# Linear attention, mixture of experts and a gelu layer on one core: one low half moved to GpSimd, one diagonal to ScalarE

## The chip, the cores and the metric

The kernel runs on one core of a Trainium2 chip. A core has TensorE (PE in the rows; its weight loads are PEld), VectorE (DVE), ScalarE (ACT), GpSimd (POOL) and SyncE (SP, which only issues DMAs here). Each engine works through its own list of instructions in order; they wait for one another by semaphores. The metric is device time in microseconds. The kernel before takes 1238.77 us, the median of three runs from 1238.41 to 1241.19.

## The reference

Three layers follow one another: softmax attention in its linear form (4 batches, 8 heads, 576 rows, head size 64), a mixture of four experts with relu (2304 rows, width 512, hidden width 1024), and a dense layer with a gelu (hidden width 2048).

```python
def _attn_ref(q, k, v) -> np.ndarray:
    q_s = q - np.max(q, axis=-1, keepdims=True)
    q_s = np.exp(q_s)
    q_s = q_s / (np.sum(q_s, axis=-1, keepdims=True) + 1e-09)
    k_s = k - np.max(k, axis=2, keepdims=True)
    k_s = np.exp(k_s)
    k_s = k_s / (np.sum(k_s, axis=2, keepdims=True) + 1e-09)
    kv = np.einsum('bhsd,bhse->bhde', k_s, v)
    return np.einsum('bhsd,bhde->bhse', q_s, kv).astype(np.float32)
...
    for e in range(E):
        h = np.maximum(x @ w1[e], 0.0)
        out += p[:, e:e + 1] * (h @ w2[e])
...
def _moe2_ref(x, w_in, w_out) -> np.ndarray:
    h = x @ w_in
    g = h * (1.0 / (1.0 + np.exp(-1.702 * h)))
    return (g @ w_out).astype(np.float32)
```

The row of key maxima, `np.max(k, axis=2)`, is a maximum over the 576 rows of a head. The expert layer's relu, `np.maximum(x @ w1[e], 0.0)`, and the gelu `g` are what the changed lines work on.

## The kernel before

All products run on TensorE in a format with a shortened mantissa, so each operand is split into a high half (a copy in that format) and a low half (the value less its high half), and each product is three: high by high, high by low, low by high. The splitting of weights, inputs and hidden activations is the work of the other three engines.

The expert layer and the gelu layer are cut into units of 256 hidden columns. The rows are in three groups of 2 x 512, 2 x 256 and 2 x 384. In the first pass of a layer the units run one after another on group 0 (`i == 0`): 13 such steps in the expert layer (the first three units are done another way) and 8 in the gelu layer. In the second pass the units run on groups 1 and 2. In a step, seven products of blocks (`m1` to `m7`, line 837) give the four tiles of the hidden activation in the manner of Strassen: `a` (from `py` or `p1`), `b` (from `u3`), `c` (from `px`) and `d` (from `pz` or `u2`). For group 0 three of the four lie in PSUM; only `b`, the tile `u` of the rows, is in SBUF: `u3c` copies `px` there by ScalarE and `u3a` adds `pz` by VectorE (line 868). Then `r` makes the high half (line 881: relu on ScalarE; in the gelu layer a gelu at 877 and a cast at 883) and `l` the low half (lines 887 and 891, both on VectorE).

The second product (`mm2`, line 954) takes eight row tiles in a step, into banks of `pso` in PSUM (`po`). VectorE adds each into `acc` (line 968, gelu layer 975 and 977), which gives the bank back. Four of the tiles of a step run at the word `TILES`, at the end of the next step, and four at `REST`, early in the step after that. Tile `b` belongs to the half of the rows that `REST` takes.

The order of work is written by hand: `STAGES` lists, for five stages, the operations of this step and (with a minus) of the one before. Between the stages stand the splits of the next unit's weights (`prepare`, lines 765 to 790: the casts on ScalarE, the sums `s` and low halves `a`, `s`, `w` on GpSimd) and, from about 125 to 310 us, turns of the attention of batches 2 and 3 (`attend2`, pumped two turns a stage). A head's turns are, for the keys: maximum `km` (474), transpose `kg` (481), `kgm` (maximum over the transposed tile 485, and the diagonal `dg` 487), `ks` (491, a product with the diagonal), `ksv` (494), `ke` (500); for the queries: `qm` (448), `qs` on GpSimd (451), `qe` (456), `qu` (sum 460, plus epsilon 461, reciprocal 462), `qn` on GpSimd (466); then `pk` (506), `t`, `px` (531). `pm`, `pb`, `pk`, `t` and `px` of the attention take banks of `pso` too.

These lines set where the changed instructions stand:

```python
"moe": (
    "-m5 -u3c m1 p1c -u3a", "m2 p1a REST", "-m6 -rc -rb -m7 -lc -u2a", "m3 u2c m4 -lb -rd ra -ld la",
    "TILES",
),
turns = ["km", "qm qs", "", "", "kg kgm", "qe", "", "", "ks ksv", "qu qn", "ke", "", "", "pk", "", "bd"]
ONE = ((("s1", "a11"), ("s2",), ("a12", "s3"), ("+s2", "+s1", "s4"), ("+s3", "a22", "+s4")),)
```

Of the kernel before, what the change touches and what calls it, by code (L numbers as in the profile page):

```python
# [8 lines left out]
F32 = mybir.dt.float32  # L9
# [5 lines left out]
AF = mybir.ActivationFunctionType  # L15
ALU = mybir.AluOpType
# [6 lines left out]
def tile_linear_attention_moe_gelu(  # L23
# [26 lines left out]
    V, S_, G, T, A = nc.vector, nc.sync, nc.gpsimd, nc.tensor, nc.scalar  # L50
# [33 lines left out]
    ident = const.tile([P, P], F32, name="ident")  # L84
# [24 lines left out]
    def copy(eng, o, i):  # L109
        (eng.copy if eng is A else eng.tensor_copy)(o, i)  # L110
# [295 lines left out]
    def attend2(b, j, c0, nc_, keys, live):  # L406
# [6 lines left out]
        y, ops = {}, {}  # L413

        def t_(n, s, tag=None):
            return pools["attn2", "p"].tile(s, F32, tag=tag or n, bufs=BUFS.get(tag or n, 2), name=f"{n}{nm}")
# [66 lines left out]
        def kgm(_):  # L483
            y["gm"] = t_("gm", [P, 1])
            V.tensor_reduce(out=y["gm"], in_=y["pm"], op=ALU.max, axis=AX.X)  # L485
            y["dg"] = t_("dg", [P, P])
            V.tensor_scalar_mul(y["dg"], ident, y["gm"])

        def ks(_):
            y["pb"] = bk("pb", [SP, 2, D])  # L490
# [48 lines left out]
        for fn in [lq, qm, qs, qe, qu, qn] + [lk, lv, km, kg, kgm, ks, ksv, ke, pk, bd] * keys:  # L539
            ops[fn.__name__] = fn  # L540
# [291 lines left out]
    def mm(ps, w, x, start, stop):  # L832
        (wh, wl), (xh, xl) = w, x
        n = 0
        for kk in range(2):
            for a, b in ((wh, xh), (wh, xl), (wl, xh)):
                T.matmul(  # L837
                    ps, a[:, kk, :], b[:, kk, :],
                    start=(start and n == 0), stop=(stop and n == 5), skip_group_check=True,
                )  # L840
                n += 1

    def mm1(g, i, m, ho):

        n = SPANS[i][1]
        nm = f"{g}_{i}"
        moe_ = units[g][0] == "moe"
        y, ops = {}, {}
        p1, u2 = ("py", "pz") if i == 0 else ("p1", "u2")
        tile_of = {"a": (0, 0, p1), "b": (1, 1, "u3"), "c": (1, 0, "px"), "d": (0, 1, u2)}  # L850

        def product(ps, w, t, first):
            def go(_):
                if first:
                    y[ps] = pools["psc", "p"].tile([P, n], F32, tag="c", name=f"{ps}{nm}")
                mm(y[ps], W1[m, w], X[i, t], first, True)

            return go

        def ev(o, ps):  # L860
            def go(eng):
                y[o] = evp.tile([P, n], F32, tag="ev", name=f"{o}{nm}")
                copy(eng or A, y[o], y[ps])

            return go

        def add(o, ps, a):
            return lambda _: V.tensor_tensor(out=y[o], in0=y[ps], in1=y[a], op=ALU.add)  # L868

        def act(x):  # L870
            ft, t, c = tile_of[x]
            s = slice(ho[t], ho[t] + n)
            hi, lo = h_hi[:, ft, s], h_lo[:, ft, s]

            def gelu(_):
                y["s" + x] = y[c] if i == 0 else evp.tile([P, n], F32, tag="ev", name=f"s{x}{nm}")
                A.activation(y["s" + x], y[c], AF.Gelu_apprx_sigmoid)

            def hi_(_):
                if moe_:  # L880
                    A.activation(hi, y[c], AF.Relu)  # L881
                else:
                    A.copy(hi, y["s" + x])

            def lo_(_):
                if moe_:
                    V.scalar_tensor_tensor(  # L887
                        out=lo, in0=y[c], scalar=0.0, in1=hi.bitcast(F32), op0=ALU.max, op1=ALU.subtract
                    )
                else:  # L890
                    V.tensor_tensor(out=lo, in0=y["s" + x], in1=hi.bitcast(F32), op=ALU.subtract)

            ops.update({"g" + x: gelu, "r" + x: hi_, "l" + x: lo_})

        if m < NPLAIN:
            def half(x, ft, kh):
                def go(_):
                    if kh == 0:
                        y["c" + x] = pools["psc", "p"].tile([P, n], F32, tag="c", name=f"c{x}{nm}")
                    b = f"b{kh + 1}{1 + (i == 'R')}"  # L900
                    mm(y["c" + x], W1[HOME.get(m, m), f"a{ft + 1}{kh + 1}"], X[0, b], kh == 0, kh == 1)

                return go

            tile_of = {"a": (0, 0, "ca"), "c": (1, 0, "cc")}
            for x, (ft, *_) in tile_of.items():
                act(x)
                ops.update({x + "1": half(x, ft, 0), x + "2": half(x, ft, 1)})
            return ops

        for x in tile_of:
            act(x)
        ops.update(
            m1=product("px", "a11", "b11", True), p1c=ev("p1", "px"),
            m2=product("py", "a12", "b21", True), p1a=add(p1, "py", "p1"),
            m3=product("px", "s2", "t2", False), u2c=ev("u2", "px"),
            m4=product("pz", "s1", "t1", True),
            m5=product("px", "s3", "t3", False), u3c=ev("u3", "px"), u3a=add("u3", "pz", "u3"),
            m6=product("px", "a22", "t4", False),
            m7=product("pz", "s4", "b22", False), u2a=add(u2, "pz", "u2"),  # L920
        )
        return ops
# [252 lines left out]
    for b, j in heads[: 2 * NPR]:  # L1175
        x = {}
# [25 lines left out]
    for k_ in range(NSTART):  # L1202
        g, i, m = steps[k_]
# [76 lines left out]
```

## Time and profile before

| what | value |
|---|---|
| median of three runs | 1238.77 us |
| the profiled execution's own time | 1240.43 us |
| its span | 1238.6 us |
| PE busy | 1210.0 us, 98% |
| DVE busy | 839.0 us, 68% |
| ACT busy | 472.8 us, 38% |
| POOL busy | 350.3 us, 28% |

The span is that of the instructions on the core; the profiled execution's own time is 1.83 us longer. TensorE is busy nearly always, and the granted clock of TensorE falls below nine tenths only in slices 7 and 8 of 40 (186 to 248 us). The busy shares of the other engines are averages over stages that differ: GpSimd does most of its work in the first third and between 840 and 1040 us. Idle time of TensorE is what can be won back; there are 28.6 us of it in the span, and time at a lower clock comes on top.

### The profile page before, as it was taken

How to read it: one execution, taken by the hardware profiler on the slowest of the kernel's cores; microseconds unless marked ns; L12 is line 12 of the kernel's file. 1: busy time of each engine (PE TensorE's matmuls, PEld its weight loads, DVE VectorE, ACT ScalarE, POOL GpSimd, SP SyncE). 2: the span in 40 equal slices, each digit the busy share in tenths (PEclk: the TensorE clock that was granted, in tenths of full speed). 3: DMA queues.
4: the chain of work that ended last, by engine and by line, in shares of the span. 5: the costliest groups of instructions: out<-in, count | busy, mean ns of one | idle time of the engine just before them, and what ended most of it. 6: DMA issues, size and time to landing. Idle time of an engine off the chain costs nothing.

```text
span 1238.6 us, 17399 instructions
## 1 busy us (share of the span) xinstructions
PE 1210.0 (98%) x6276; PEld 1047.6 (85%) x6276; DVE 839.0 (68%) x1392; ACT 472.8 (38%) x1034; POOL 350.3 (28%) x389
## 2 busy tenths in 40 slices
PE   8999998899999999999999999999999999999998
PEld 7778776678888899998899988998788889899987
DVE  7864777775566848988988975576345676554554
ACT  6544443343343353222222322236444543333332
POOL 5424654455464001111111431025353600000000
PEclk9999998899999999999999999999999999999999
DMA  9845965555647466666656532534656655333333
GB/s 205 232 160 170 316 198 167 169 192 178 233 164 269 136 196 197 210 184 224 213 188 221 188 109 96 183 124 163 236 182 235 234 183 161 111 106 107 110 104 85
DMA packets 132406, 221.13 MB, mean 179 GB/s; under 512 B 30176, under 2 KB 61920, under 8 KB 131680
## 3 DMA queue, kind: packets, MB, share of 16 engines
q1 hardware_dynamic: 119936, 212.94, 53.6%
q10 hardware_dynamic: 12384, 7.08, 1.9%
q8 instruction: 50, 0.82, 0.3%
q14 instruction: 36, 0.29, 0.1%
HBM read 133.21 MB, written 86.77 MB: 178 GB/s over the span
## 4 chain that ended last, share of the span: by engine, by line
PE 84%; DVE 8%; DMA 4%; issue 2%; POOL 1%; ACT 1%; SPq 0%; ACTq 0%; POOLq 0%
PE po L954 42%; PE px L837 20%; PE pz L837 10%; PE py L837 5%; DVE h_lo L887 2%; DMA w64o<-in_moe_w_out 2%; DVE acc L968 1%; PE pk L506 1%; PE p L378 1%; DMA x_ffn<-xt 1%; PE cc_L L837 1%; PE ca_L L837 1%; PE cc_R L837 1%; PE ca_R L837 1%; PE px L358 1%
## 5 line engine op out<-in xcount | busy, mean ns | idle before, releaser
L954 PE MATMUL po<-w,h_hi 128*128 128x512 f32 x1728 | 539.8, 394 | 7.7 <-DVE gm L485 5.1
L954 PEld LDWEIGHTS po<-w,h_hi 128*128 128x128 f32 x1728 | 321.7, 189 | 72.3 <-DVE gm L485 5.5
L954 PE MATMUL po<-w,h_lo 128*128 128x512 f32 x864 | 339.3, 393 | 1.8 <-DVE h_lo L887 1.8
L968 DVE SCALAR_TENSOR_TENSOR acc<-po,pr,acc 128x512 f32<-128x512 f32 x270 | 195.3, 745 | 77.0 <-PE po L954 76.6
L954 PEld LDWEIGHTS po<-w,h_lo 128*128 128x128 f32 x864 | 163.1, 189 | 37.5 <-DVE h_lo L887 2.7
L110 ACT COPY u<-px 128x384 f32<-128x384 f32 (+2 forms) x138 | 65.2, 473 | 202.7 <-PE px L837 200.6
L977 DVE TENSOR_TENSOR acc<-po,acc 128x512 f32<-128x512 f32 x126 | 85.8, 689 | 60.8 <-PE po L954 60.7
L777 POOL TENSOR_TENSOR a<-ra,a 128x256 fp32r<-128x256 f32 x69 | 54.1, 784 | 163.9 <-ACT a L771 158.0
L868 DVE TENSOR_TENSOR u<-pz,u 128x256 f32<-128x256 f32 (+2 forms) x117 | 61.0, 521 | 54.7 <-ACT u L110 54.6
L777 POOL TENSOR_TENSOR s<-s,s 128x256 fp32r<-128x256 f32 x94 | 73.5, 790 | 62.7 <-ACT s L771 45.0
L881 ACT ACTIVATE h_hi<-px 128x256 fp32r<-128x256 f32 (+2 forms) x45 | 21.8, 483 | 141.1 <-PE px L837 141.0
L887 DVE SCALAR_TENSOR_TENSOR h_lo<-u,h_hi 128x256 fp32r<-128x256 f32 (+2 forms) x77 | 65.6, 870 | 7.5 <-ACT h_hi L881 7.2
L790 POOL TENSOR_TENSOR w<-rc,w 128x512 fp32r<-128x512 f32 x46 | 60.3, 1310 | 29.4 <-ACT w L784 29.3
L824 POOL TENSOR_TENSOR doi<-doi,dti 128x512 f32<-128x512 f32 x16 | 21.1, 1318 | 161.2 <-DVE doi L821 141.3
L765 POOL TENSOR_TENSOR s<-ra 128x256 f32<-128x256 f32 x48 | 39.7, 829 | 77.7 <-DMA ra<-wi 53.1
L824 POOL TENSOR_TENSOR doo<-doo,dto 128x512 f32<-128x512 f32 x16 | 21.3, 1331 | 99.0 <-DVE doo L821 92.3
L110 ACT COPY p<-px 128x384 f32<-128x384 f32 (+2 forms) x69 | 32.9, 477 | 34.2 <-PE px L837 34.0
L771 ACT CAST s<-s 128x256 fp32r<-128x256 f32 x96 | 37.3, 414 | 22.4 <-POOL s L765 12.9
L887 DVE SCALAR_TENSOR_TENSOR h_lo<-px,h_hi 128x256 fp32r<-128x256 f32 (+2 forms) x45 | 24.5, 545 | 31.1 <-ACT h_hi L881 31.0
L881 ACT ACTIVATE h_hi<-u 128x256 fp32r<-128x256 f32 (+2 forms) x77 | 38.2, 496 | 3.7 <-DVE u L868 3.7
L868 DVE TENSOR_TENSOR p<-py,p 128x256 f32<-128x256 f32 (+1 forms) x48 | 23.4, 486 | 18.4 <-PE py L837 18.4
L771 ACT CAST a<-ra 128x256 fp32r<-128x256 f32 x75 | 30.2, 406 | 12.4 <-DMA ra<-wi 5.3
(329 smaller groups left out, 2494.0 us busy)
## 6 DMA issues: line engine op xcount, KB each, us to landing
w<-k_w SPq DMA_DIRECT2D x50, 512.0 KB, 5.0
k_w<-w SPq DMA_DIRECT2D x48, 512.0 KB, 5.4
k_s<-s SPq DMA_DIRECT2D x84, 256.0 KB, 5.5
s<-k_s SPq DMA_DIRECT2D x84, 256.0 KB, 3.3
a<-k_a SPq DMA_DIRECT2D x76, 256.0 KB, 2.7
k_a<-a SPq DMA_DIRECT2D x73, 256.0 KB, 4.9
ra<-in_moe_w SPq DMA_DIRECT2D x19, 512.0 KB, 4.7
rc<-in_moe_w SPq DMA_DIRECT2D x16, 512.0 KB, 6.3
```

The lines of the kernel that those rows point to most:

```text
L110: (eng.copy if eng is A else eng.tensor_copy)(o, i)
L771: A.copy(W1[m, x][0], block_w(m, x))
L777: eng.tensor_tensor(out=lo, in0=block_w(m, x), in1=hi.bitcast(F32), op=ALU.subtract)
L790: eng.tensor_tensor(out=lo, in0=raw[m, 1][:, c, :], in1=hi.bitcast(F32), op=ALU.subtract)
L824: G.tensor_tensor(out=o, in0=o, in1=t.bitcast(F32), op=ALU.add)
L837: T.matmul(ps, a[:, kk, :], b[:, kk, :], start=(start and n == 0), stop=(stop and n == 5), skip_group_check=True,)
L868: return lambda _: V.tensor_tensor(out=y[o], in0=y[ps], in1=y[a], op=ALU.add)
L881: A.activation(hi, y[c], AF.Relu)
L887: V.scalar_tensor_tensor(out=lo, in0=y[c], scalar=0.0, in1=hi.bitcast(F32), op0=ALU.max, op1=ALU.subtract)
L954: T.matmul(ps, a, b, start=(n == 0), stop=(n == 3 * FT - 1))
L968: V.scalar_tensor_tensor(out=acc[ti], in0=ps, scalar=pe, in1=acc[ti], op0=ALU.mult, op1=ALU.add)
L977: V.tensor_tensor(out=acc[ti], in0=ps, in1=acc[ti], op=ALU.add)
```

## The change

Two things change. In the attention of batches 2 and 3, the diagonal `dg` (identity times the key maxima) is made by ScalarE instead of VectorE, 8 times. In the steps of group 0, the low half of tile `b` is made by GpSimd, 21 times. GpSimd subtracts without a relu, so in the expert layer (13 of the 21) ScalarE first makes the relu in place in `u` and then the high half as a copy of it: two instructions where there was one.

```diff
--- before.py
+++ after.py
@@ -484,7 +484,7 @@
             y["gm"] = t_("gm", [P, 1])
             V.tensor_reduce(out=y["gm"], in_=y["pm"], op=ALU.max, axis=AX.X)
             y["dg"] = t_("dg", [P, P])
-            V.tensor_scalar_mul(y["dg"], ident, y["gm"])
+            A.mul(y["dg"], ident, y["gm"])
 
         def ks(_):
             y["pb"] = bk("pb", [SP, 2, D])
@@ -876,14 +876,21 @@
                 y["s" + x] = y[c] if i == 0 else evp.tile([P, n], F32, tag="ev", name=f"s{x}{nm}")
                 A.activation(y["s" + x], y[c], AF.Gelu_apprx_sigmoid)
 
+            by_g = i == 0 and x == "b"
+
             def hi_(_):
-                if moe_:
+                if moe_ and by_g:
+                    A.activation(y[c], y[c], AF.Relu)
+                    A.copy(hi, y[c])
+                elif moe_:
                     A.activation(hi, y[c], AF.Relu)
                 else:
                     A.copy(hi, y["s" + x])
 
             def lo_(_):
-                if moe_:
+                if by_g:
+                    G.tensor_tensor(out=lo, in0=y[c] if moe_ else y["s" + x], in1=hi.bitcast(F32), op=ALU.subtract)
+                elif moe_:
                     V.scalar_tensor_tensor(
                         out=lo, in0=y[c], scalar=0.0, in1=hi.bitcast(F32), op0=ALU.max, op1=ALU.subtract
                     )
```

The places below show how the lists of instructions move. The new lines shift numbers: 887 becomes 894, 968 becomes 975, 881 becomes 886, and the new instructions are on lines 883, 884 (relu and copy) and 892.

The first place is GpSimd's list in the step at about 176 to 200 us: `w` is the second weight's low half, `v`, `qn` and `q` belong to the attention, `s` and `a` to the next unit's first weight. Before:

```order
L790 TENSOR_TENSOR w_9_2079<-rc_1738,w_9_2079 128x512
L437 MEMSET v_0_0_2087 96x6
L466 TENSOR_TENSOR qn_2_0_2112<-q_2_0_1691,qu_2_0_2108 96x2x6x64
L451 TENSOR_TENSOR q_3_0_1870<-q_3_0_1870,qm_3_0_2114 96x768
L777 TENSOR_TENSOR s_10_2137<-s_10_2045,s_10_2137 128x256
L777 TENSOR_TENSOR s_10_2141<-s_10_1974,s_10_2141 128x256
L765 TENSOR_TENSOR s_10_2145<-ra_1947,s_10_2045 128x256
L790 TENSOR_TENSOR w_9_2147<-rc_1738,w_9_2147 128x512
```

and after:

```order
L790 TENSOR_TENSOR w_9_2082<-rc_1739,w_9_2082 128x512
L437 MEMSET v_0_0_2090 96x6
L466 TENSOR_TENSOR qn_2_0_2115<-q_2_0_1692,qu_2_0_2111 96x2x6x64
L451 TENSOR_TENSOR q_3_0_1872<-q_3_0_1872,qm_3_0_2117 96x768
L892 TENSOR_TENSOR h_lo<-u_0_1964,h_hi 128x512
L777 TENSOR_TENSOR s_10_2140<-s_10_2047,s_10_2140 128x256
L777 TENSOR_TENSOR s_10_2144<-s_10_1976,s_10_2144 128x256
L765 TENSOR_TENSOR s_10_2148<-ra_1949,s_10_2047 128x256
L790 TENSOR_TENSOR w_9_2150<-rc_1739,w_9_2150 128x512
```

The subtraction stands behind the two attention instructions and ahead of the weight sums of the next unit.

The second place is VectorE's list in the same step: `qu` and `qm` are of two heads, `acc` takes the tiles of `TILES`. Before:

```order
L461 TENSOR_SCALAR qu_2_0_2108<-qu_2_0_2108 96x12
L462 RECIPROCAL qu_2_0_2108<-qu_2_0_2108 96x12
L448 TENSOR_REDUCE qm_3_0_2114<-q_3_0_1870 96x12
L887 SCALAR_TENSOR_TENSOR h_lo<-u_0_1962,h_hi 128x512
L887 SCALAR_TENSOR_TENSOR h_lo<-pz_0_1842,h_hi 128x512
L887 SCALAR_TENSOR_TENSOR h_lo<-py_0_2005,h_hi 128x512
L968 SCALAR_TENSOR_TENSOR acc_0_775<-po_0_2158,pr,acc_0_775 128x512
L968 SCALAR_TENSOR_TENSOR acc_1_781<-po_1_2166,pr,acc_1_781 128x512
L968 SCALAR_TENSOR_TENSOR acc_2_818<-po_2_2174,pr,acc_2_818 128x512
L968 SCALAR_TENSOR_TENSOR acc_3_830<-po_3_2182,pr,acc_3_830 128x512
L485 TENSOR_REDUCE gm_3_0_2213<-pm_3_0_2211 128x1
L487 TENSOR_SCALAR dg_3_0_2215<-ident,gm_3_0_2213 128x128
```

and after:

```order
L461 TENSOR_SCALAR qu_2_0_2111<-qu_2_0_2111 96x12
L462 RECIPROCAL qu_2_0_2111<-qu_2_0_2111 96x12
L448 TENSOR_REDUCE qm_3_0_2117<-q_3_0_1872 96x12
L894 SCALAR_TENSOR_TENSOR h_lo<-pz_0_1844,h_hi 128x512
L894 SCALAR_TENSOR_TENSOR h_lo<-py_0_2007,h_hi 128x512
L975 SCALAR_TENSOR_TENSOR acc_0_775<-po_0_2161,pr,acc_0_775 128x512
L975 SCALAR_TENSOR_TENSOR acc_1_781<-po_1_2169,pr,acc_1_781 128x512
L975 SCALAR_TENSOR_TENSOR acc_2_818<-po_2_2177,pr,acc_2_818 128x512
L975 SCALAR_TENSOR_TENSOR acc_3_830<-po_3_2185,pr,acc_3_830 128x512
L485 TENSOR_REDUCE gm_3_0_2216<-pm_3_0_2214 128x1
```

The low half of `u` is gone from ahead of the other two low halves and the four additions, and the diagonal from behind `gm`.

The third place is ScalarE's list in the step before, at about 144 to 154 us: `ke` and `q` are exponentials of the attention, `a` and `w` weight casts. Before:

```order
L500 ACTIVATE ke_0_0_1740<-k_0_0_1414 96x2x6x64
L456 ACTIVATE q_1_0_1533<-q_1_0_1533 96x768
L881 ACTIVATE h_hi<-px_0_1510 128x512
L881 ACTIVATE h_hi<-u_0_1717 128x512
L771 CAST a_9_1818<-ra_1687 128x256
L784 CAST w_8_1825<-rc_1529 128x512
```

and after:

```order
L500 ACTIVATE ke_0_0_1741<-k_0_0_1414 96x2x6x64
L487 ACTIVATE dg_1_0_1793<-ident,gm_1_0_1791 128x128
L456 ACTIVATE q_1_0_1533<-q_1_0_1533 96x768
L886 ACTIVATE h_hi<-px_0_1510 128x512
L883 ACTIVATE u_0_1718<-u_0_1718 128x512
L884 CAST h_hi<-u_0_1718 128x512
L771 CAST a_9_1820<-ra_1688 128x256
L784 CAST w_8_1827<-rc_1529 128x512
```

The diagonal stands between the two exponentials, and the high half of `u` is now a relu in place and a cast.

## Rows read from the trace of the kernel before

**Rows 1.** Waits of PE: engine, line, releaser; us in total, times, longest us.
```profile
PE px L531 <- DVE acc L968: 5.8, 3, 3.9
PE po L954 <- DVE gm L485: 5.1, 1, 5.1
```

**Rows 2.** Busy time by stretch: length, the five engines, granted clock, DMA share, GB/s.
```profile
187.90:192.00 4.10, 0.19 (x1) 0.00 (x0) 4.10 (x5) 0.40 (x1) 4.10 (x5) 0.81 0.26 53
192.00:196.50 4.50, 4.47 (x16) 3.80 (x17) 2.75 (x5) 1.24 (x2) 0.79 (x2) 0.50 1.01 359
217.20:222.30 5.10, 0.01 (x1) 0.00 (x0) 5.07 (x5) 0.99 (x3) 4.95 (x6) 0.89 0.29 73
222.30:228.20 5.90, 5.90 (x14) 4.64 (x15) 2.05 (x4) 0.00 (x0) 0.73 (x1) 0.52 1.00 340
900.00:1000.00 100.00, 100.00 (x443) 82.84 (x442) 56.42 (x85) 48.90 (x102) 48.31 (x60) 1.00 0.62 223
```

**Rows 3.** Timeline of DVE, 183 to 213 us: start, us, line, operation.
```profile
183.74 6.37 DVE L887 SCALAR_TENSOR_TENSOR h_lo<-u,h_hi 128x512 fp32r<-128x512 f32 x1
...
191.24 2.71 DVE L968 SCALAR_TENSOR_TENSOR acc<-po,pr,acc 128x512 f32<-128x512 f32 x4
...
212.68 8.20 DVE L887 SCALAR_TENSOR_TENSOR h_lo<-u,h_hi 128x512 fp32r<-128x512 f32 x1
```

**Rows 4.** Timeline of POOL, 183 to 191 us.
```profile
183.09 1.73 POOL L466 TENSOR_TENSOR qn<-q,qu 96x768 f32<-96x768 f32 x1 [1.57 <-DVE qu L462]
184.78 1.47 POOL L451 TENSOR_TENSOR q<-q,qm 96x768 f32<-96x768 f32 x1
...
189.51 1.19 POOL L777 TENSOR_TENSOR s<-s,s 128x256 fp32r<-128x256 f32 x1
```

**Rows 5.** Instructions by source line: duration ns min/median/max, first and last start.
```profile
L887 DVE SCALAR_TENSOR_TENSOR h_lo<-u,h_hi x13: 624/1240/8201, 132.3 to 421.7; 128x512 fp32r<-128x512 f32 x13
L887 DVE SCALAR_TENSOR_TENSOR h_lo<-py,h_hi x13: 673/680/692, 114.2 to 404.0; 128x512 fp32r<-128x512 f32 x13
L891 DVE TENSOR_TENSOR h_lo<-u,h_hi x8: 680/681/683, 870.7 to 1017.0; 128x512 fp32r<-128x512 f32 x8
L487 DVE TENSOR_SCALAR dg<-ident,gm x8: 285/287/717, 131.8 to 282.8; 128x128 f32<-128x128 f32 x8
L461 DVE TENSOR_SCALAR qu<-qu x8: 169/170/397, 143.8 to 295.8; 96x12 f32<-96x12 f32 x8
L790 POOL TENSOR_TENSOR w<-rc,w x46: 1257/1296/1748, 25.4 to 1001.8; 128x512 fp32r<-128x512 f32 x46
L777 POOL TENSOR_TENSOR s<-s,s x94: 717/742/1810, 99.0 to 986.6; 128x256 fp32r<-128x256 f32 x94
L784 ACT CAST w<-rc x48: 605/623/652, 24.7 to 1001.1; 128x512 fp32r<-128x512 f32 x48
```

**Rows 6.** Timeline of PE: attention product, then REST, behind the first stall.
```profile
192.03 1.33 PE L531 MATMUL px<-qT,kvbd 128*128 128x288 f32 x2 [3.94 <-DVE acc L968]
...
200.74 0.62 PE L954 MATMUL po<-w,h_hi 128*128 128x512 f32 x2
```

**Rows 7.** Timeline of POOL and of DVE, 159 to 162 us.
```profile
159.22 1.29 POOL L790 TENSOR_TENSOR w<-rc,w 128x512 fp32r<-128x512 f32 x1
161.70 0.17 DVE L461 TENSOR_SCALAR qu<-qu 96x12 f32<-96x12 f32 x1
```

**Rows 8.** Timeline of ACT, DVE and PE, 147 to 181 us.
```profile
147.21 0.85 ACT L456 ACTIVATE q<-q 96x768 f32<-96x768 f32 x1 [1.39 <-POOL q L451]
152.43 0.60 ACT L881 ACTIVATE h_hi<-px 128x512 fp32r<-128x512 f32 x1 [4.37 <-PE px L837]
180.79 0.59 ACT L110 COPY u<-px 128x512 f32<-128x512 f32 x1 [0.97 <-PE px L837]
150.53 0.29 DVE L487 TENSOR_SCALAR dg<-ident,gm 128x128 f32<-128x128 f32 x1
156.58 0.38 PE L491 MATMUL pb<-dg,ones 128*96 128x128 f32 x2
```

## The prediction made before the run

> **What bounds the kernel now.** I read the waits of TensorE first, then busy time by stretch, then the timelines of VectorE and GpSimd where TensorE stands still. TensorE is busy 98% of the span, so a change off its path is worth nothing except where TensorE waits or runs at a lower clock. The waits name two large ones, both on VectorE: 3.9 us for `acc` and 5.1 us for `gm` [rows 1]. The stretches place them: TensorE does 0.19 us of work between 187.9 and 192.0, and 0.01 us between 217.2 and 222.3 [rows 2]. Behind each, the granted clock is at the lower of its two levels (0.50 is 1.2 of 2.4 GHz): 0.50 for 4.5 us and 0.52 for 5.9 us [rows 2]. VectorE is "busy" all through both stalls, but with one instruction: the low half of `u`, 6.37 us the first time and 8.20 us the second [rows 3]. The same form from PSUM (`py`) takes 673 to 692 ns in all 13 cases, and the low half of `u` itself takes 680 to 683 ns in the gelu layer; only the 13 of the expert layer run from 624 to 8201 ns [rows 5]. So the work is 0.68 us and the rest is a wait. For what: GpSimd works without a gap from 183.09 on, through the whole stall (4.10 of 4.10 us), and at 189.51 one of its instructions takes 1.19 us, where the median of its like is 742 ns; 0.6 us later VectorE's instruction is done [rows 2 to 5]. I read this as VectorE being kept out of SBUF by GpSimd, for an operation with both inputs in SBUF, until GpSimd leaves a gap. Behind it in order stand the additions that give TensorE its banks (191.24 us, [rows 3]).
>
> The Trainium skill, "SBUF — State Buffer", section "Who interferes with whom", says that a VectorE instruction with two SBUF inputs contends with a GpSimd instruction that reads SBUF, and that the one that starts first holds the shared pair for its whole instruction. Taken to the letter, the wait would be one GpSimd instruction, at most 1.73 us here [rows 4]. The trace agrees that they contend, but the wait of 6.37 us goes over several instructions; there the measurement decides.
>
> **The change part by part.** The sum is made against the profiled execution, 1240.43 us; the median is 1.66 us below it, and I take the difference off the median.
>
> *The low half of `u` leaves VectorE (13 in the expert layer).* First stall: VectorE goes from `qm`, which ends at 183.74, straight to the low halves of `pz` and `py` (2 x 0.68 us) and the first addition (0.75 us, a quarter of the 2.71 us and some overlap): done near 186, when TensorE still has tiles until 187.9. So its 3.94 us of waiting go, and the slow stretch behind goes with it: 4.5 x (1 - 0.50) = 2.25 us [rows 2, 6]. Second stall: without the 8.20 us, two low halves and `gm` end near 215, before the bank is asked for at 217.2. That gives back 5.09 us, and 5.9 x (1 - 0.52) = 2.8 us of slow clock [rows 1, 2]. Sum: 3.94 + 2.25 + 5.09 + 2.8 = 14.1 us. What is late next: nothing that I find. In the first, the other two banks come back as the tiles end; in the second, VectorE has idle time between its additions.
>
> *Two small stalls.* Of the 5.8 us for `acc`, 5.8 - 3.94 = 1.9 us are two stalls near 163 and 278 us [rows 1]. Before each, the low half of `u` took longer on VectorE than its 0.68 us, so one would book the gain. I book nothing: in that step GpSimd has the weight sums and `w` between the new subtraction and `qn`, its run ends 1.3 us later than at 160.5 [rows 7] and some 0.6 us later again for ScalarE's extra instruction. VectorE reaches the scalar addition on `qu` (line 461) about 1 us earlier, inside this run. That operation too has waited for GpSimd once: 397 ns against 170 [rows 5]. So the wait moves from the one to the other. From -1.9 us (all gone) to +0.6 us (both a little longer); I take 0.
>
> *GpSimd gets 21 subtractions.* The nearest row is `w`, of the same shape, both inputs in SBUF: 1257 to 1748 ns, median 1296 [rows 5]; 21 x 1.3 = 27 us on an engine that is busy 28%. Cover: tile `b` is wanted only at `REST`. In the worst place, the first stall's step, the subtraction stands behind `qn` and `q`, which end at 184.78 + 1.47 = 186.25; so it is done near 187.6. `REST` started at 200.74 and TensorE resumed at 192.03 [rows 6]; resumed at 187.9 at full clock it reaches `REST` at 187.9 + 8.7 - 2.25 = 194.4. 6.8 us of slack. What is queued behind it on GpSimd (weights of the next unit and the raw buffers that they free) is wanted a step later, 20 us or more; a weight load that lands 1.3 to 2 us later holds up a cast on ScalarE at a time when its next work for TensorE is some us away. In the gelu layer the subtraction falls into idle time of GpSimd and TensorE is 100 of 100 us busy [rows 2]: no gain from the 8 x 0.68 us [rows 5], and no loss. Bounds: 0 to 1.5 us if a subtraction comes late once; I take 0.
>
> *ScalarE gets 13 relus and 8 diagonals.* A relu in place is like `w`'s cast, 605 to 652 ns [rows 5], and the copy behind it waits for it: some 0.7 us, 13 times. It pushes back a weight cast and the copy of `px`, which had 0.97 us of idle ahead in the first stall's step [rows 8] and whose reader on TensorE (`m5`) comes after `TILES`. The diagonal has a quarter of the cast's columns and so takes less than 0.65 us. It makes ScalarE wait for `gm`, with an exponential queued behind it. At 150 us this is tightest: the diagonal can start when VectorE did it, 150.53, ScalarE stood idle for 4.37 us before 152.43, and diagonal and exponential (0.65 + 0.85 us) fit in between [rows 8]. TensorE wants the diagonal 6 us later, at 156.58 [rows 8]. From 0 to 1 us; I take 0.
>
> *VectorE loses 8 diagonals* of 0.29 to 0.72 us [rows 5]: nothing that TensorE waits for.
>
> Total: -14.1 us. 1240.43 - 14.1 = 1226.3 for an execution like the profiled one, 1238.77 - 14.1 = 1224.7 for the median.
>
> **The rivals.**
>
> *One stall only.* In one of the two places something else is late once VectorE is free (a bank held by the attention, ScalarE waiting for a later weight load). For it: both steps are packed with attention work. Against: in the timelines the banks come back in time. Then 6.2 or 7.9 us: 1232.6 or 1230.9.
>
> *The port explains only one instruction.* If a wait for GpSimd is at most one of its instructions, the rest of the 6.37 and 8.20 us has another cause and meets the next operation on VectorE. Then some 1.5 us at each place goes: 1235.8. By the page named above this is how it would go. Against: the additions behind ran back to back at once.
>
> *No net change.* The banks are late for another reason, or the wait goes whole to line 461: 1238.8.
>
> *Slower.* The mechanism is line 461 in the three steps in which GpSimd's `qn` stands behind the second `w`. There the run on GpSimd is now longer by the subtraction: 1.3 + 3 x 0.74 + 1.3 = 4.8 us of work without a gap [rows 5]. If line 461 is kept out for the whole of it each time, TensorE stalls for about 4 us and runs some 4 us at half clock: 6 us x 3 = 18 us against the 14.1: 1242.7. It decides from about 3 us of waiting each. The same page says that a scalar operation from SBUF to SBUF contends too. For it: the 397 ns, and the diagonal's 285 to 717 ns [rows 5]. Against: line 461 releases `qn`, so GpSimd is idle in front of it as soon as its run is over (1.57 us in the first stall's step, [rows 4]), and it comes late in the run.
>
> **How the numbers follow.** Both stalls go: 0.70, at 1221 to 1228. One only: 0.13. One instruction only: 0.05. No net change: 0.05. Slower: 0.07. A measurement of this kernel can tell 0.2%, 2.5 us, from no change. Faster: 0.70 + 0.13 + 0.03 = 0.86; same: 0.05 + 0.02 = 0.07; slower 0.07. For eight in ten I go from 1221, where the small stalls go too, to 1233, which takes in the cases of one stall.
>
> **What would show it.** In the profile after: no wait of TensorE over 2 us between 150 and 300 us; the granted clock full there; no VectorE instruction of the `h_lo` lines above 0.7 us in the first pass; the subtraction on GpSimd 1.25 to 1.75 us and always done before `REST`; the stalls near 163 and 278 us still about 1 us each, with line 461 above 170 ns ahead of them. A long wait that remains with VectorE "busy" in another single instruction would prove the forecast wrong, and a stall of TensorE on `h_lo` of GpSimd the costing of the cover.

## The result, and the profile after

The changed kernel takes 1222.93 us (median of 4 runs, 1221.92 to 1224.86), the kernel before 1238.74 us (4 runs on the same chip, 1238.41 to 1241.19). The ratio is 0.987, with a 95% interval of 0.9851 to 0.9889. The profiled execution after took 1223.91 us, 16.5 us less than the profiled one before (1240.43); 14.1 us were forecast.

Waits of TensorE in the kernel after (engine, line, releaser; us in total, times, longest us):

```profile
PE px L531 <- DVE acc L975: 2.0, 2, 1.0
...
PE pz L837 <- DVE h_lo L894: 1.7, 2, 1.2
```

Both large waits of [rows 1] are gone: no wait of 3.9 us for `acc`, none of 5.1 us for `gm`. What is left for `acc` is two waits of 1.0 us, the small ones near 163 and 278 us before, now at 161.86 and 261.83.

Busy time by stretch, kernel after (columns as in [rows 2]; the last two are longer stretches that are also read below):

```profile
187.90:192.00 4.10, 4.10 (x22) 3.43 (x21) 1.13 (x4) 2.56 (x6) 2.96 (x4) 1.00 0.56 117
192.00:196.50 4.50, 4.50 (x22) 3.72 (x21) 2.60 (x6) 0.41 (x1) 2.18 (x4) 1.00 1.05 361
...
180.00:240.00 60.00, 59.48 (x295) 49.38 (x294) 40.02 (x68) 28.62 (x65) 38.86 (x47) 1.00 0.62 192
132.90:140.00 7.10, 7.10 (x34) 5.87 (x33) 5.31 (x8) 4.20 (x11) 7.10 (x9) 1.00 1.12 323
```

The same two stretches before:

```profile
180.00:240.00 60.00, 50.49 (x219) 40.71 (x218) 46.98 (x58) 19.14 (x41) 29.11 (x34) 0.89 0.55 171
132.90:140.00 7.10, 7.10 (x27) 5.71 (x27) 4.33 (x7) 3.82 (x10) 7.10 (x9) 0.80 1.10 319
```

Where TensorE stood for 4.10 us and then ran at half its clock for 4.5 us [rows 2], it is now busy throughout at the granted clock 1.00. The work has moved forward by some 6 to 9 us behind the first stall, so equal windows don't hold equal work; the 60 us window takes in both places: TensorE's busy time in it went from 50.49 to 59.48 us, the clock from 0.89 to 1.00, and 295 records stand where 219 stood.

The gain can be counted. TensorE's waits between 100 and 300 us were 5.8 + 5.1 + 2.6 + 0.9 = 14.4 us and are 2.0 + 1.7 + 0.8 = 4.5 us: 9.9 us. The slow clock gave back 2.25 and 2.8 us behind the two stalls as forecast, and 7.1 x (1 - 0.80) = 1.4 us in a third stretch, 132.9 to 140.0. Together 16.4 of the 16.5 us. That they meet so closely is in part luck. By the two pages TensorE's idle time fell from 28.6 to 17.4 us and its busy time from 1210.0 to 1204.7: 11.2 and 5.3 us. So 1.3 us more of waiting went than these 200 us show, and 1.2 us less came back from the slow clock than the three stretches give.

Timeline of the kernel after around the place of the first stall (start, us, engine, line, operation):

```profile
181.15 0.89 DVE L448 TENSOR_REDUCE qm<-q 96x12 f32<-96x768 f32 x1
181.96 0.67 DVE L894 SCALAR_TENSOR_TENSOR h_lo<-pz,h_hi 128x512 fp32r<-128x512 f32 x1
...
183.15 1.39 DVE L975 SCALAR_TENSOR_TENSOR acc<-po,pr,acc 128x512 f32<-128x512 f32 x2
182.75 1.47 POOL L451 TENSOR_TENSOR q<-q,qm 96x768 f32<-96x768 f32 x1
184.18 1.29 POOL L892 TENSOR_TENSOR h_lo<-u,h_hi 128x512 fp32r<-128x512 f32 x1
192.18 0.61 PE L961 MATMUL po<-w,h_hi 128*128 128x512 f32 x2
```

VectorE goes from `qm` straight to the low halves of `pz` and `py` and to the additions, which began at 191.24 before [rows 3] and begin at 183.15 now. The subtraction on GpSimd stands where the argument put it, behind `qn` and `q`, ends at 185.47, and `REST` asks at 192.18: 6.7 us of slack, forecast 6.8.

Instructions by line, kernel after (ns min/median/max, first and last start):

```profile
L892 POOL TENSOR_TENSOR h_lo<-u,h_hi x21: 1284/1293/1318, 135.3 to 999.8; 128x512 fp32r<-128x512 f32 x21
L487 ACT ACTIVATE dg<-ident,gm x8: 399/402/405, 131.9 to 267.0; 128x128 f32<-128x128 f32 x8
L883 ACT ACTIVATE u<-u x13: 619/623/624, 129.9 to 401.9; 128x512 f32<-128x512 f32 x13
L461 DVE TENSOR_SCALAR qu<-qu x8: 168/205/1142, 141.9 to 279.3; 96x12 f32<-96x12 f32 x8
```

The three new costs are those forecast: 1.29 us for a subtraction (the median of `w` was 1296 ns, [rows 5]), 0.40 us for a diagonal on ScalarE (under 0.65 was forecast), 0.62 us for a relu (605 to 652 ns). Line 461, 170 ns before and 397 at most [rows 5], now takes up to 1142 ns.

### The profile page after: what moved, and what is told of

It is laid out like the page before. It is cut to its first block, busy times and chain, and to the rows that moved or that the text cites. A ratio compares the mean times of both kernels' runs of the same rounds, so it can differ in the third digit from the quotient of the medians.

```text
span 1222.1 us, 17422 instructions
## 1 busy us (share of the span) xinstructions
PE 1204.7 (99%) x6276; PEld 1046.2 (86%) x6276; DVE 810.7 (66%) x1363; ACT 482.8 (40%) x1055; POOL 373.2 (31%) x410
## 4 chain that ended last, share of the span: by engine, by line
PE 88%; DVE 5%; DMA 3%; issue 2%; POOL 1%; ACT 1%; SPq 0%; ACTq 0%; POOLq 0%
PE po L961 44%; PE px L837 21%; PE pz L837 10%; PE py L837 5%; DVE acc L975 1%; DVE h_lo L894 1%; PE hot L1174 1%; PE pk L506 1%; PE p L378 1%; DMA x_ffn<-xt 1%; PE cc_L L837 1%; PE ca_L L837 1%; PE cc_R L837 1%; PE ca_R L837 1%; PE px L531 1%
## 5 line engine op out<-in xcount | busy, mean ns | idle before, releaser
L892 POOL TENSOR_TENSOR h_lo<-u,h_hi 128x512 fp32r<-128x512 f32 x21 | 27.2, 1297 | 68.3 <-ACT h_hi L888 41.7
L894 DVE SCALAR_TENSOR_TENSOR h_lo<-u,h_hi 128x256 fp32r<-128x256 f32 (+1 forms) x64 | 38.0, 615 | 7.2 <-ACT h_hi L886 6.8
```

Source lines behind the costliest of these rows:

```text
L894: V.scalar_tensor_tensor(out=lo, in0=y[c], scalar=0.0, in1=hi.bitcast(F32), op0=ALU.max, op1=ALU.subtract)
```

## The experiments

Twelve runs were made, of nine new kernels; the kernel before and the kernel after ran once more, and one kernel twice. Those of a group ran on one chip beside the kernel before; each group has its own times of before, and ratios are made within a group. A row of GpSimd means its instructions from one idle stretch to the next. Theory A is the prediction's: a VectorE instruction whose inputs both lie in SBUF stands still while GpSimd's reading instructions follow each other without a gap.

### First group: the parts alone

The kernel before took 1232.49 us here (26 runs, 1229.12 to 1238.53): on this chip its runs lie far apart, and lower than elsewhere. The fourth group bears on why.

*The low half moved, the diagonal left on VectorE.*

```diff
 (against the kernel after)
-            A.mul(y["dg"], ident, y["gm"])
+            V.tensor_scalar_mul(y["dg"], ident, y["gm"])
```

> The low half of the third tile on GpSimd as in the changed kernel, the diagonal back on VectorE. Theory A (the two stalls near 190 and 220 us are VectorE's low half kept out of SBUF by GpSimd's run): the whole gain stays, 14 to 16 us below before, 1223 to 1225 us, and no wait of TensorE over 2 us between 150 and 300 us. Rival B (the diagonal on ScalarE has a share, since it too has both its input and its output in SBUF and stood 0.72 us on VectorE): part of the gain is missing, 1226 to 1232 us.

1231.0 us (1229.73 to 1234.77), ratio 0.9975 (0.9953 to 0.9997). The expectation fell; the time lies in the range of its rival B. The profiled execution is the slowest of the ten, 1234.77 us. Its timeline:

```profile
131.26 0.10 POOL L437 MEMSET v<- 96x6 f32 x1
131.32 1.46 POOL L451 TENSOR_TENSOR q<-q,qm 96x768 f32<-96x768 f32 x1
132.33 10.53 DVE L487 TENSOR_SCALAR dg<-ident,gm 128x128 f32<-128x128 f32 x1
...
136.11 1.29 POOL L892 TENSOR_TENSOR h_lo<-u,h_hi 128x512 fp32r<-128x512 f32 x1
...
142.01 0.71 POOL L777 TENSOR_TENSOR s<-s,s 128x256 fp32r<-128x256 f32 x1
142.68 0.10 POOL L437 MEMSET v<- 96x6 f32 x1
144.72 0.74 PE L491 MATMUL pb<-dg,ones 128*96 128x128 f32 x2 [6.03 <-DVE acc L975]
```

The two old stalls are gone, as the theory wants, but the diagonal, 0.29 us of work, now stands for 10.53 us. From 131.32 to 142.72 GpSimd runs 13 reading instructions back to back, the moved subtraction among them, and the diagonal is done when its small memset comes. Behind that memset GpSimd is idle until 150.32, so whether the memset let it in or the end of the row is not told apart here. TensorE waits 6.03 us, and from 144.7 to 150.0 its granted clock is 0.50. The wait is not removed by the first part alone; it goes to the next VectorE instruction that reads and writes SBUF only.

*The diagonal moved, the low half left on VectorE.*

```diff
 (against the kernel before)
-            V.tensor_scalar_mul(y["dg"], ident, y["gm"])
+            A.mul(y["dg"], ident, y["gm"])
```

> Only the diagonal on ScalarE, the low half on VectorE as before. Theory A: both stalls of 4 to 5 us stay, with a low half of 6 to 8 us ahead of each; 1238 to 1240 us. Rival B: several us below before, 1230 to 1236 us.

1233.28 us (1225.04 to 1237.97), ratio 0.9989 (0.9962 to 1.0017): no change in the median, with a wide spread. The 1238 to 1240 us expected were meant beside a kernel before of 1238.7; here it took 1232.49. The profiled execution is its fastest one, 1225.04 us:

```profile
180.77 1.62 DVE L887 SCALAR_TENSOR_TENSOR h_lo<-u,h_hi 128x512 fp32r<-128x512 f32 x1
180.12 1.72 POOL L466 TENSOR_TENSOR qn<-q,qu 96x768 f32<-96x768 f32 x1 [1.57 <-DVE qu L462]
181.80 1.92 POOL L451 TENSOR_TENSOR q<-q,qm 96x768 f32<-96x768 f32 x1
...
203.12 6.28 DVE L887 SCALAR_TENSOR_TENSOR h_lo<-u,h_hi 128x512 fp32r<-128x512 f32 x1
```

At the first place the low half was let in after 1.62 us, between two GpSimd instructions, and the second of these took 1.92 us where it took 1.47 before [rows 4]. At the second place it stood 6.28 us, and TensorE waited 3.19 us, with the clock at 1.00 behind. So VectorE can be let in between two reading instructions too, and the spread of the times suggests that this differs between executions of one program.

*The form: relu in place, then a plain subtraction, still on VectorE.*

```diff
 (against the kernel after)
-                    G.tensor_tensor(out=lo, in0=y[c] if moe_ else y["s" + x], in1=hi.bitcast(F32), op=ALU.subtract)
+                    V.tensor_tensor(out=lo, in0=y[c] if moe_ else y["s" + x], in1=hi.bitcast(F32), op=ALU.subtract)
```

> The changed kernel with all 21 low halves of the third tile back on VectorE, as a subtraction with both inputs in SBUF (the relu is already in place); relu in place, copy and diagonal stay on ScalarE. Theory A: the long low halves come back (5 us and more at two places) and with them both stalls: 1237 to 1242 us. Rival C (what was slow on VectorE is the form with relu and subtraction in one instruction, not SBUF against GpSimd): the subtraction takes 0.7 us each time and the gain stays, 1222 to 1226 us.

1241.07 us (1233.6 to 1242.54), ratio 1.0047 (1.0024 to 1.0071): slower than before. Timeline of VectorE in it:

```profile
130.28 9.63 DVE L892 TENSOR_TENSOR h_lo<-u,h_hi 128x512 fp32r<-128x512 f32 x1
...
186.83 6.37 DVE L892 TENSOR_TENSOR h_lo<-u,h_hi 128x512 fp32r<-128x512 f32 x1
...
216.91 6.29 DVE L892 TENSOR_TENSOR h_lo<-u,h_hi 128x512 fp32r<-128x512 f32 x1
```

The form of the instruction is not the cause. It met three long GpSimd rows where the profile before had two; what moved it into the first of them, the relu or the diagonal's leaving, was not separated.

*The expert layer alone* (the gelu layer's eight subtractions go back to VectorE).

```diff
 (against the kernel after)
-            by_g = i == 0 and x == "b"
+            by_g = moe_ and i == 0 and x == "b"
```

> The changed kernel, but in the gelu layer (8 of the 21) the low half stays on VectorE. Theory A: no difference from the changed kernel, 1222 to 1225 us: TensorE does not wait there, and the 0.68 us on VectorE are hidden either way. Rival D (a share of the gain comes from the gelu layer, or a loss is hidden there): 2 us or more away from the changed kernel.

1223.35 us (1221.25 to 1223.58), ratio 0.9907 (0.9873 to 0.9942). The changed kernel itself did not run on this chip; elsewhere it took 1222.93 and 1221.23 us, so no sign that the gelu layer gives or takes anything, as forecast. With this kernel for the whole change, the two parts don't add: the low half alone gives 1.5 us, the diagonal alone nothing beyond the noise (0.8 us slower), both together 9.1.

### Second group: what lets VectorE in

The kernel before: 1237.79 us (7 runs, 1236.77 to 1242.44).

*Nothing moved; a GpSimd instruction that only writes.* A memset of a tile that nobody uses, 0.46 us, behind each subtraction of `q`.

```diff
 (against the kernel before)
+            G.memset(spare, 0.0)        # 128x432, behind line 451
...
-    pools["edge", "p"].tile([P, 432], F32, name="edge")
+    spare = pools["edge", "p"].tile([P, 432], F32, name="edge")
+    G.memset(spare, 0.0)
```

> The kernel before, with one more instruction on GpSimd: a memset of 128x432 of an unused tile behind each of the 8 instructions that subtract the query maxima (line 451). GpSimd has more work, but a break in its run in which it reads nothing from SBUF. Theory A1 (VectorE's low half waits for an instruction of GpSimd that does not read SBUF): it gets in at the memset, so near 186 us instead of 190 in the first stall, and within 2 us of its start in the second; both stalls mostly go: 1224 to 1231 us, although nothing left VectorE. Rival A2 (it waits for GpSimd to have nothing to do, whatever GpSimd does): the low halves stay at 6 to 8 us or grow by the memset: 1238 to 1243 us.

1225.29 us (1223.54 to 1225.89), ratio 0.9896 (0.9879 to 0.9912). Timeline of this kernel at the first place:

```profile
182.03 3.29 DVE L888 SCALAR_TENSOR_TENSOR h_lo<-u,h_hi 128x512 fp32r<-128x512 f32 x1
183.07 1.47 POOL L451 TENSOR_TENSOR q<-q,qm 96x768 f32<-96x768 f32 x1
184.48 0.46 POOL L454 MEMSET edge<- 128x432 f32 x1
184.90 1.71 POOL L778 TENSOR_TENSOR s<-s,s 128x256 fp32r<-128x256 f32 x2
...
206.05 2.70 DVE L888 SCALAR_TENSOR_TENSOR h_lo<-u,h_hi 128x512 fp32r<-128x512 f32 x1
207.06 0.46 POOL L454 MEMSET edge<- 128x432 f32 x1
208.16 1.18 POOL L766 TENSOR_TENSOR s<-ra 128x256 f32<-128x256 f32 x1
```

The low half is done at 185.32, just behind the memset, and GpSimd's next pair then takes 1.71 us against 1.42 for the same pair in the kernel after. At the second place it took 2.70 us (within 2 was expected), and there it did not get in at the memset: that ends at 207.52, one more instruction that reads follows it, and the low half is done at 208.75, beside the reading instruction that takes 1.18 us instead of 0.73. More work on GpSimd, nothing taken from VectorE, and most of the gain is there: what stands in GpSimd's row decides the stalls. That it is the gap can be read at the first place alone.

*The same place, with an instruction that reads.* A copy of 128x216 in place of the memset, 0.36 us.

```diff
+            G.tensor_copy(spare[:, :216], spare[:, 216:])
```

> The same, with a copy of 128x216 inside the unused tile in place of the memset: an instruction of about the same place and size that reads SBUF. Theories A1 and A2 both: it gives VectorE no way in; the low halves stay at 6 us or more in at least one of the two places, 1236 to 1243 us. If e5 and this run are both fast, the shift in time or any added instruction is enough, and reading has no part in it.

1231.33 us (1228.91 to 1232.45), ratio 0.9946 (0.9931 to 0.9961). Timeline:

```profile
182.19 6.68 DVE L888 SCALAR_TENSOR_TENSOR h_lo<-u,h_hi 128x512 fp32r<-128x512 f32 x1
184.64 0.36 POOL L454 COPY edge<-edge 128x216 f32<-128x216 f32 x1
188.26 1.19 POOL L778 TENSOR_TENSOR s<-s,s 128x256 fp32r<-128x256 f32 x1
...
212.45 2.61 DVE L888 SCALAR_TENSOR_TENSOR h_lo<-u,h_hi 128x512 fp32r<-128x512 f32 x1
214.48 1.17 POOL L766 TENSOR_TENSOR s<-ra 128x256 f32<-128x256 f32 x1
```

At the first place the copy lets nobody in: 6.68 us, over it and four more instructions, until one of GpSimd's takes 1.19 us instead of 0.73. At the second place VectorE got in after 2.61 us, again at an instruction that took 0.45 us more than its like, and at the same instruction as in the kernel with the memset. So at the second place any added instruction was enough, as the expectation's last sentence has it, and the 1236 to 1243 us expected were missed: one stall went. At the first place memset and copy differ, and so do the times, by 6.0 us: the four runs of the one (1223.54 to 1225.89) lie below the four of the other (1228.91 to 1232.45). Between two reading instructions VectorE is sometimes let in, and where this happens shifts with the row. Why there and not earlier, the records don't say.

*The small waits: without line 461*, which adds 1e-9 to sums that are at least 1 (a term is exp(0)).

```diff
 (against the kernel after)
-            V.tensor_scalar_add(y["qu"], y["qu"], EPS)
```

> The changed kernel without line 461 (it leaves out the addition of 1e-9 to the query sums, which are at least 1). Theory A: the two stalls of 1.00 and 0.97 us that are left near 162 and 262 us are line 461 waiting for GpSimd's run, which the new subtraction made longer; without it the first goes or falls under 0.3 us and the second too: 1 to 2 us below the changed kernel, 1220.5 to 1222.5 us. Rival E (the chain of VectorE's attention work alone makes them): both stay near 0.9 us, 1222 to 1224 us.

1221.12 us (1218.55 to 1222.16), ratio 0.9863 (0.9848 to 0.9878). TensorE's two waits for `acc` are gone; the third group repeats it.

*Twice the subtraction on GpSimd.* Each of the 21 subtractions is made a second time, to the same place.

```diff
 (against the kernel after)
+                    G.tensor_tensor(out=lo, in0=y[c] if moe_ else y["s" + x], in1=hi.bitcast(F32), op=ALU.subtract)
```

> The changed kernel with each of the 21 subtractions issued twice on GpSimd, one behind the other: 27 us more on GpSimd. Theory A: the cover holds 1.3 us more, since the low half is wanted 4 to 7 us later than it is done; within 1.5 us of the changed kernel, 1222 to 1225 us. Rival F (GpSimd is nearly late, and TensorE begins to wait for it): 1.3 us a step in several of the 13 steps, 1227 to 1240 us.

1222.84 us (1221.76 to 1224.29), ratio 0.988 (0.9866 to 0.9895). The changed kernel did not run on this chip; its ratios were 0.987 and 0.986. Beside them 21 x 1.3 = 27 us more on GpSimd cost nothing that can be measured: the cover of 6.7 us holds. Line 461 at the first small stall, in this kernel:

```profile
158.55 0.53 DVE L461 TENSOR_SCALAR qu<-qu 96x12 f32<-96x12 f32 x1
```

The row ahead is longer, and yet line 461 takes 0.53 us instead of 1.14 in the kernel after, and TensorE waits 0.38 us instead of 1.00. In the kernel after it ends at 160.08, at the end of the one instruction that it met (`w`, 158.72 to 160.01); here at 159.08, again at the end of the instruction that it met. So at this place line 461 waits for one instruction, not for the row.

### Third group: a better version, and the gap for the diagonal

The kernel before: 1238.06 us (7 runs, 1236.5 to 1241.61).

> The changed kernel once more, as the partner of the next run. Theory A (VectorE's two-input instruction stands still for as long as GpSimd's reading instructions follow each other without a gap): no VectorE instruction of line 487 is left, line 461 still has a 96x12 addition of about 1.1 us at about 159 us and its 0.75 us wait of TensorE behind it; ratio to before about 0.987. If the gain was an accident of one chip, the ratio comes out above 0.993.

The changed kernel (no edit): 1221.23 us (1220.56 to 1222.74), ratio 0.986 (0.9839 to 0.988).

> The changed kernel without line 461, which adds 1e-9 to sums that are at least 1, beside the changed kernel itself on one chip. Theory A: TensorE's two waits of 0.75 and 0.46 us behind line 461 (at 162 and 262 us) are gone, and the time is 1 to 2 us (0.1 to 0.15%) below the changed kernel's. Rival (those waits are hidden, or the next VectorE instruction stands in the same place): within 0.5 us of the changed kernel, with a reduction or reciprocal of line 460 or 462 of about 1 us in the place of line 461's.

The edit is that of the kernel without line 461. 1220.23 us (1219.18 to 1221.69), ratio 0.9854 (0.9834 to 0.9874). The 0.75 and 0.46 us that the two expectations call waits are not: at both places the product behind takes 0.75 us, and the waits are 1.00 and 0.97 us. Timelines of the two, the changed kernel first:

```profile
158.33 1.14 DVE L461 TENSOR_SCALAR qu<-qu 96x12 f32<-96x12 f32 x1
161.24 0.75 PE L531 MATMUL px<-qT,kvbd 128*128 128x288 f32 x2 [1.00 <-DVE acc L975]
```

```profile
156.86 0.94 DVE L460 TENSOR_REDUCE qu<-q 96x12 f32<-96x768 f32 x1
157.84 0.22 DVE L461 RECIPROCAL qu<-qu 96x12 f32<-96x12 f32 x1
```

Without the addition nothing on VectorE takes its place (line 461 is the reciprocal there), and TensorE doesn't wait. The medians differ by 1.0 us, in the direction and about the size expected, but the intervals overlap: the waits are shown to go, the gain in time is not told apart from none. This kernel has the lowest median of all.

*The low half moved, the diagonal on VectorE, and a memset behind each subtraction.*

```diff
 (against the kernel of the first experiment)
+                    G.memset(spare, 0.0)        # 128x432, behind line 892
```

> The first experiment (low half on GpSimd, diagonal left on VectorE) with one more GpSimd instruction behind each of the 21 subtractions: a memset of 128x432 of a tile that nobody uses, 0.46 us, which reads nothing. In the first experiment the diagonal stood still from 132.33 us for 10.53 us, over a GpSimd row in which the subtraction of 136.11 us ended at 137.40. Theory A1 (a GpSimd instruction that reads nothing lets VectorE in): the diagonal ends beside that memset, so the longest of line 487 is about 5.5 us, TensorE's 6.03 us wait for line 491 falls below 1.5 us, and the time is 1222 to 1226 us. Rival (what holds VectorE is the length of GpSimd's row, whatever stands in it): the longest of line 487 is 10 to 11.5 us, the wait 6 to 7 us, the time 1230 to 1233 us.

1225.85 us (1225.18 to 1226.89), ratio 0.9899 (0.9881 to 0.9918). Timeline:

```profile
131.81 9.85 DVE L487 TENSOR_SCALAR dg<-ident,gm 128x128 f32<-128x128 f32 x1
136.46 0.46 POOL L893 MEMSET edge<- 128x432 f32 x1
136.52 5.13 DVE L895 SCALAR_TENSOR_TENSOR h_lo<-pz,h_hi 128x512 fp32r<-128x512 f32 x1
137.12 4.53 DVE L895 SCALAR_TENSOR_TENSOR h_lo<-py,h_hi 128x512 fp32r<-128x512 f32 x1
137.72 3.94 DVE L976 SCALAR_TENSOR_TENSOR acc<-po,pr,acc 128x512 f32<-128x512 f32 x4
141.54 0.72 POOL L777 TENSOR_TENSOR s<-s,s 128x256 fp32r<-128x256 f32 x1
141.78 0.46 PE L491 MATMUL pb<-dg,ones 128*96 128x128 f32 x2 [3.62 <-DVE acc L976]
```

Neither theory as it was put. VectorE moves on at the memset: the next instruction starts 0.06 us after it, and the two behind at the usual 0.60 us. But the diagonal and the three rows behind it all end at 141.65 to 141.66, and TensorE waits 3.62 us (6.03 without the memset). The diagonal's 9.85 us speaks for the rival, the 136.52 for the theory, and the time lies in the theory's range; what held the four ends together stays open. The diagonal is also another form than the low half, a scalar operation with one tensor input instead of two; whether that is why the memset did not let it end was not tested.

### Fourth group: the kernel before once more

> The kernel before, unchanged, profiled a second time. Its profiled execution so far had the low half of u at 6.37 us (183.74) and 8.20 us (212.68) and took 1240.43 us. Theory A with a grant that varies from one execution to the next: each of the two is either about 1 to 3 us long, and then one of GpSimd's instructions beside its end is 0.3 to 0.5 us longer than its like, or 6 to 8.5 us; the time goes with the number of long ones, about 1239 us with two, 1231 to 1234 us with one, 1225 to 1227 us with none. Rival (the scatter between runs has another cause, such as when the weights arrive): both are 6 to 8.5 us long whatever the time.

No edit. 1237.41 us (11 runs, 1231.52 to 1239.53), beside 13 others of the same kernel with 1237.39 us (1228.94 to 1242.08), ratio 1.0017 (0.9994 to 1.004). The execution that was profiled is the fastest, 1231.52 us. Timeline:

```profile
182.39 1.62 DVE L887 SCALAR_TENSOR_TENSOR h_lo<-u,h_hi 128x512 fp32r<-128x512 f32 x1
183.43 1.92 POOL L451 TENSOR_TENSOR q<-q,qm 96x768 f32<-96x768 f32 x1
...
204.75 8.21 DVE L887 SCALAR_TENSOR_TENSOR h_lo<-u,h_hi 128x512 fp32r<-128x512 f32 x1
212.36 1.18 POOL L777 TENSOR_TENSOR a<-ra,a 128x256 fp32r<-128x256 f32 x1
```

The same program as in [rows 3], the same instruction at the same place: 1.62 us here, 6.37 there. VectorE was let in ahead of `q`, which then took 1.92 us against 1.47 [rows 4]; the first stall is absent, the second stands with 8.21 us. The time, 1231.5 us, is the one expected with one stall. So the first stall of the kernel before comes or stays away from one execution to the next. Two profiles show this; that it makes up the whole spread of the times is likely and not shown. The number of long low halves alone doesn't give the time: the execution of 1225.04 us in the first group had one of 6.28 us. The changed kernel's runs lie within 3 us of each other on either chip.

## Why the prediction was right, and where it was not

*The two stalls* (3.94 + 2.25 and 5.09 + 2.8 us): right in place, cause and size. The waits are gone, the clock behind them is 1.00, and that GpSimd's row is the cause is shown by the memset, which removes most of both with nothing moved. "Until GpSimd leaves a gap" says too much: it is borne out by the memset at the first place and where the row ends (9.63 and 10.53 us). In the kernel before itself VectorE got in beside a reading instruction with more of them behind it without a gap (189.51 us, 1.19 us long, [rows 4]; 220.28 us, 1.18 us long). What I had not seen is that a stall can come and go between executions: the one profile showed both, and the medians before of 1237 to 1239 us in all groups but the first suggest that most runs there have both. So there was luck in the size: on the first group's chip, where the kernel before took 1232.49 us, the change without its gelu part gave 9.1 us and not 14.1.

*The 2.4 us beyond the sum.* They are not in either stall. At 131.06 us TensorE waited 2.12 us for `h_lo` before and 1.18 at 130.82 after: 0.94 us, and the 1.4 us of slow clock behind (as far as the sum above can be divided so finely). Ahead of it a load of expert weights released GpSimd's row at 129.37 us before and at 129.14 after, before any moved instruction matters. The second profile of the kernel before has the wait of 2.1 us there too, but the clock at 1.00 behind it; the kernel without line 461 has 2.1 us in one profile and 1.0 in the other; the four kernels of the first two groups that leave the low half on VectorE have 1.0. So the small gain there is not one of the moved instructions; it differs between executions of one program.

*The small stalls* (0 booked): right, and the wait did move to line 461. It takes 1.14 us in the step in which the low half took 1.73 us before, and TensorE waits its 1.0 us as ever; taking line 461 away removes both waits. The later end of GpSimd's row is not what sets its length: with a row 1.3 us longer still it took 0.53 us, to the end of the instruction that it met. The rival that made the change slower by it wanted some 3 us each, for the whole row; the longest was 1142 ns.

*The cover on GpSimd and ScalarE* (0): right. 6.7 us of slack, and a second subtraction is hidden too.

*"VectorE loses 8 diagonals ...: nothing that TensorE waits for"*: this step failed. By the trace of before it was true, since the longest diagonal took 717 ns. But with the low half gone the diagonal is the next VectorE instruction with SBUF on both sides, and it stands behind a GpSimd run that the new subtraction makes 1.3 us longer. Left on VectorE it costs TensorE 6.03 us of waiting, 2.65 us more by the clock behind (5.3 us at 0.50), and 7.65 us of time on one chip (1231.0 against the 1223.35 of the expert layer alone, medians). The total came out because the change moves both parts; the sum credited all of it to the first. I had asked of line 461 where the wait goes next, and not of line 487.

*The rival of one instruction.* It held that the wait would meet the next operation on VectorE. In the kernel after it doesn't, beyond line 461. But with the diagonal left there it does, and not for the rival's reason, another cause behind one instruction: the diagonal is kept out by the same row, for 13 instructions. What the change avoids, by moving both parts, is that the wait goes on to the next operation.

The Trainium skill, "SBUF — State Buffer", section "Who interferes with whom", says that the form with two SBUF inputs contends with GpSimd instructions that read SBUF and not with those that only write, and that a scalar operation from SBUF to SBUF can contend too, in a mode that takes both ports. The runs agree: 3.29 us with the memset against 6.68 with the copy at the first place, 10.53 us for the diagonal, 1.14 us for line 461. That the one kept out waits for one instruction holds for line 461 and not for the others: 10.53 us is a row of 13 instructions of at most 1.46 us, and there the measurement decides.

## What to carry to other kernels

When a VectorE instruction is "busy" many times its usual duration while GpSimd works without a gap, count the wait, not the work, and ask of every later VectorE instruction with all its operands in SBUF whether it will stand there instead: on one chip, moving one alone gave 1.5 us, both 9.1. Where no engine has room to take it, a short GpSimd instruction that reads nothing, put into the long row, gave 12.5 us where the whole change gave some 16 on other chips; one that reads gave 6.5. Add to a gain on TensorE the slow clock behind the stall: it was 5 us beside 9 of waiting. Look whether it is there: behind waits of 3.94, 5.09 and 6.03 us the clock fell to 0.50, behind those of 3.19 and 3.62 it stayed at 1.00. And profile a kernel twice before calling a stall its own.

## What the runs showed of the hardware

A 0.29 us VectorE instruction was kept out for 10.53 us by a GpSimd row of instructions of 0.7 to 1.5 us; it ended at a memset of 0.10 us, behind which GpSimd was idle. A scalar operation on 96x12 elements (line 461) waited only for the one instruction that it met, 1.14 and 0.53 us. One program lets it in early or late from one execution to the next (1.62 and 6.37 us at the same place), and the GpSimd instruction beside which it got in was 0.29 to 0.46 us longer. And a gap can be enough for the next instructions to start and not for their ends: four rows that started between 131.81 and 137.72 us ended together at 141.66.
